# Q's weight load cut into single row chunks, and the fifth column group projected tile by tile

## The chip, the cores and the metric

The kernel runs on one core of a Trainium2 chip. The time is device microseconds (us) of one execution. One execution was also recorded by the hardware profiler; its rows give start and length of every instruction, measured from the first one. The engines are PE (matmuls; PEld is its weight load), DVE (vector), ACT (scalar), POOL (GpSimd) and SP (which here only issues DMA transfers). ACT and POOL can issue transfers too; each issuing engine has its own queue. Every engine works through its own list of instructions in order, and waits on semaphores for the others.

## The reference

One input `x` (2048 rows, 640 columns, bf16) is normalised row by row, and three terms are added:

```python
xn = layernorm(x)                       # (x - mean) / sqrt(var + 1e-5)
# A: attention, 32 heads of 20 columns, window of 8 keys at distance 2
q, k, v = split(xn @ wqkv)              # wqkv: 640 x 1920
logits[h, s, w] = q[h, s] . k[h, s - 2 * w] * 20 ** -0.5    # w = 0..7; s - 2w < 0 is masked
A = (softmax over w of logits, times v[h, s - 2 * w]) @ wo
# B: a bilinear unit
B = ((xn @ w_gate) * (xn @ w_up)) @ w_down                  # 640 x 1536, 1536 x 640
out = x + A + B
```

## The kernel before

**Tiles.** Rows are worked on in 16 tiles of 128 and, in most matmuls, in 4 blocks `j` of 512. The 640 input columns are five row chunks `c` of a weight matrix (128 rows each), and the 640 output columns of Q or K are five column groups `m` of 128 (the columns `m`, `m+5`, ...), so that Q of one tile is 5 x 5 matmuls of 128 columns.

**The normal head.** For tile `t`, `front(t)` makes statistics of the two halves on DVE (L600), the mean and variance (L603), the square root on ACT (L610), its reciprocal on DVE (L617), and the normalised rows `XNS` (L627 on DVE for tiles 0 to 5, L630 on ACT after that). These are transposed to `XNT`: tiles 2 and 3 by PE (L658) and a DVE copy (L664), all others by a transposing DMA (L673). A tile that is ready is marked `xnt`.

**The shortcut for tiles 0 and 1.** To start PE before the normalisation is done, these two tiles are only centred (L695), transposed on PE (L705), copied to `XRAW` by ACT (L716, in two parts: chunks 0 and 1, chunks 2 to 4), and multiplied with Q's and K's weights as they are (`raw_group`, L755, chunk by chunk). The result `RAW` is copied out by ACT (L764) and scaled by row on POOL later (L808).

**The loads at the head** are written out by hand (L1642 to L1655): x of tile 0 in two halves (SP and ACT), x of tile 1, Q's chunks 0 to 2 in one transfer of 480 KB from ACT's queue, Q's chunks 3 and 4 in one of 320 KB from SP's, then K's chunks in two, with x of tiles 2, 3 and 4 between and behind. ACT then loads its table and runs one square root (L1654), and PE runs nine warm-up matmuls (and three more after tile 0's transposes).

**Projections.** `proj_group` multiplies up to four column groups of Q or K for a stretch of rows into one PSUM bank (L838) and lets ACT copy them out (L843). For tiles 2 and 3 the column groups 0 to 3 are done tile by tile; group 4 is done for both tiles together, once for Q and once for K. Then follow V of block 0, and Q, K and V of the later rows. After them come the attention logits (products on DVE L996 and L1045, sums on PE L1128), gate and up (L1430), the weighted values (L1307 on DVE, L1312 on POOL, sums on PE L1366), and the output matmuls (L1531 and L1582).

**What sets the order.** Nothing but the head is ordered by hand. Each piece of work is a `Task` with a priority (smaller is earlier); `Sched.run` keeps an assumed time per engine, takes the assumed cost of each operation (`occ`) and, for the loads at the head, an assumed landing time (`land`), and always emits the task of highest priority among those that could start soon on some engine. `have(...)` holds a chain of tasks until a mark is set. So a changed load, landing time or gate makes the whole order be worked out anew, and each engine's list is fixed when the program is built; on the chip the lists are followed in order whatever the real times are.

Of the kernel before, what the change touches and what calls it, by code (L numbers as in the profile page):

```python
# [11 lines left out]
NCH = 5  # L12
# [9 lines left out]
TS = 128  # L22
# [335 lines left out]
def build_kernel(nc, A_x, A_wqkv, A_wo, B_x, B_w_gate, B_w_up, B_w_down, out):  # L358
    K = Sched(nc)
# [108 lines left out]
    def mark(*k):  # L468
        done.add(k)

    def bump(*k):
        count[k] = count.get(k, 0) + 1

    def have(*k):
        return lambda: k in done
# [7 lines left out]
    def dma(o, i, r=(), w=(), name="", eng="sp", group=None, land=None):  # L483
        n = mybir.dt.size(o.dtype)
        for s in o.shape:
            n *= s
        return op(eng, lambda e: e.dma_start(o, i), r=r, w=w, dma=True, name=name, nbytes=n, group=group, land=land)  # L487
# [27 lines left out]
    def x_load(t, eng="sp", land=None):  # L515
        dma(XST[:, xslot(t), :], xhbm[t * TS:(t + 1) * TS, :], w=[XST[:, xslot(t), :]], name=f"xld{t}", eng=eng, land=land)
        mark("x", t)
# [9 lines left out]
    def wqkv_load(g, lo=0, hi=NCH, eng="sp", land=None):  # L527
        dst = WQKV[:, WPOS[g], lo:hi, :]
        dma(dst, wqkv_src[:, lo:hi, g * D:(g + 1) * D], w=[dst], name=f"ld_wqkv{g}_{lo}", eng=eng, land=land)
# [62 lines left out]
    def front(t):  # L592
# [5 lines left out]
        def stats(i):  # L598
            o, a = st[:, 6 * i:6 * i + 6], x[:, i * DHALF:(i + 1) * DHALF]
            op("dve", lambda e: e.bn_stats(o, a), r=[a], w=[("st", t, i)], name=f"bn{t}_{i}", occ=0.49)  # L600
# [32 lines left out]

        yield have("x", t)
        for i in range(2):
            if t == 4 and i == 1 or t == 5 and i == 0:
                yield have("xnt", 3)
            yield Task("dve", lambda: stats(i), r=[x[:, i * DHALF:(i + 1) * DHALF]] if t == 0 else [x], prio=p)
        yield Task("dve", aggr, r=[("st", t, 1)], prio=p)
# [185 lines left out]
    def wcols(which, c, m):  # L825
        if which == 2:
            return WQKV[:, WPOS[2], c, m * 128:(m + 1) * 128]
        return WQKV[:, WPOS[which], c, m:D:NCH]

    def mms(parts, b, name, outer=None):  # L830
        order = [(p, c) for p in parts for c in range(NCH)]
        if outer is not None:
            order = [(p, c) for c in outer for p in parts]
        for k, ((o, which, m, s0, n), c) in enumerate(order):
            if True:
                first = c == 0
                l, x = wcols(which, c, m), XNT[:, c, s0:s0 + n]
                op("pe", (lambda o, l, x, c, first: lambda e: e.matmul(o, l, x, start=first, stop=(c == NCH - 1)))(o, l, x, c, first),  # L838
                   r=[l, x], w=[o], name=f"{name}_{m}_{c}", occ=n / 2400 + 0.0024, lat=0.3)

    def evac(parts, name):
        for o, i, n in parts:
            X = op("act", (lambda o, i: lambda e: e.activation(o, i, ACT.Copy))(o, i), r=[i], w=[o], name=name,  # L843
                   occ=0.12 + n * 0.9e-3)
        return X

    def qk_dst(which, m0, nm, s0, n):
        if which == 1:
            return KT[:, m0:m0 + nm, PAD + s0:PAD + s0 + n]
        j, i = divmod(s0, JB)  # L850
        return QT[:, j, m0:m0 + nm, i:i + n]

    def bank_view(b, col, nm, n):
        return PS[:, b, col:col + nm * n].rearrange("p (m s) -> p m s", m=nm)

    def proj_group(items, s0, n, prio, keys):
        hold = []

        def go(b):
            parts, outs, col = [], [], 0  # L860
            for which, m0, nm in items:
                for k in range(nm):
                    parts.append((PS[:, b, col + k * n:col + (k + 1) * n], which, m0 + k, s0, n))
                outs.append((qk_dst(which, m0, nm, s0, n), bank_view(b, col, nm, n), nm * n))
                col += nm * n
            mms(parts, b, f"p{items[0][0]}_{s0}")
            hold.append((b, outs))

        def ev():
            b, outs = hold[0]  # L870
            X = evac(outs, f"pev{items[0][0]}_{s0}")
            K.free_bank(b, X)
            for which, m0, nm in items:
                for k in range(nm):
                    for u in range(n // TS):
                        bump("qk", which, (s0 + u * TS) // JB, m0 + k)

        yield Task("pe", go, r=[wcols(items[0][0], NCH - 1, 0), XNT[:, NCH - 1, s0 + n - TS:s0 + n]], prio=prio, banks=1)
        yield Task("act", ev, r=[o for _, o, _ in hold[0][1]], prio=5)

    def proj_qk():
        for t in (2, 3):
            yield have("xnt", t)
            for which in (0, 1):
                K.spawn(proj_group([(which, 0, 4)], t * TS, TS, 10, None))
        for which in (0, 1):
            K.spawn(proj_group([(which, 4, 1)], 2 * TS, 2 * TS, 10.2, None))
        for t in (4, 6):
            yield have("xnt", t + 1)
            for items in ([(0, 0, 2)], [(1, 0, 2)], [(0, 2, 2)], [(1, 2, 2)], [(0, 4, 1), (1, 4, 1)]):  # L890
                if 1 not in QUAD or items[0][0] or items[0][1] == 4:
                    K.spawn(proj_group(items, t * TS, 2 * TS, 11 + t * 0.1, None))
        for j in (2, 3):
            yield have("xnt", 4 * j + 3)
            for m in range(NCH):
                for which in (0, 1):
                    if which or j not in QUAD or m == NCH - 1:
                        K.spawn(proj_group([(which, m, 1)], j * JB, JB, 12 + j, None))
# [743 lines left out]
    x_half(0, 3.05)  # L1642
    x_half(1, 3.25, eng="act")
    x_load(1, land=4.4)
    wqkv_load(0, 0, 3, eng="act", land=5.55)
    wqkv_load(0, 3, NCH, land=6.65)
    wqkv_load(1, 0, 2, land=7.5)
    x_load(2, land=7.95)
    wqkv_load(1, 2, NCH, land=9.3)
    x_load(3, land=9.75)  # L1650
    x_load(4, land=10.2)
    mark("kloads")
    K.t["act"] = 3.0
    op("act", lambda e: e.activation(MV[:, 0, 7:8], EPSC[:, 0:1], ACT.Sqrt), r=[EPSC[:]], w=[("sdx",)], name="table", occ=0.25)  # L1654
    warm(9, JB)  # L1655

# [13 lines left out]
    for t in range(NT):  # L1670
        K.spawn(front(t))
    for t in range(N_RAW):
        K.spawn(raw(t))
    K.spawn(proj_qk())
    K.spawn(products())
    for j in range(NJ):
# [16 lines left out]
def bass_parallel_sum__sliding_local_dilated__glu_gated_bilinear__prompt_kernel(  # L1693
    nc, A_x, A_wqkv, A_wo, B_x, B_w_gate, B_w_up, B_w_down, out
):
    build_kernel(nc, A_x, A_wqkv, A_wo, B_x, B_w_gate, B_w_up, B_w_down, out)
# [28 lines left out]
```

## Time and profile before

| | us |
|---|---|
| median of 3 runs | 264.66 (264.48 to 265.0) |
| profiled execution, its own time | 265.61 |
| its span, first to last instruction | 263.9 |
| PE busy | 259.0 |
| DVE busy | 219.3 |
| POOL busy | 166.5 |
| ACT busy | 112.7 |
| PE's first matmul with Q's weights | 7.14 after the start |

A line of a group names the line of the kernel, the engine, the operation and the tiles (output, then inputs). In the chain of work that ended last, each line is a start, a length and what ran or was waited for; a `q` behind an engine's name is its issuing part. In the list of waits a line says who waited for whom, and then the time in total, how often, and the longest.

### The profile page before, as it was taken

Reading aid. Unit: us, or ns where it says so; the run is one execution under the profiler, and the core shown is the slowest. Engines: PE = TensorE matmul, PEld = TensorE weight load, DVE = VectorE, ACT = ScalarE, POOL = GpSimd, SP = SyncE. Lnnn points to the kernel's source line nnn. Section 1 sums busy time; section 2 is a strip of 40 time slices with the busy share of each in tenths; the row PEclk is TensorE's granted clock in tenths of the full one; section 3 lists DMA queues with packets and bytes.
Section 4 is the critical chain, followed back from the end, with each engine's and each line's share of the span. In section 5 each row is a group of like instructions: output and inputs, shape, how many; then the busy total and the mean of one; then the engine's idle time right before and its main releaser. Section 6 shows DMA issues by size and latency. Waiting matters only on the chain.

```text
span 263.9 us, 4105 instructions
## 1 busy us (share of the span) xinstructions
PE 259.0 (98%) x1586; PEld 135.8 (51%) x1586; DVE 219.3 (83%) x260; ACT 112.7 (43%) x199; POOL 166.5 (63%) x101
## 2 busy tenths in 40 slices
PE   6999999999999999999999999999999999999996
PEld 2996974444444444444444444444444444445675
DVE  5587899999988897679878999999989989995041
ACT  3378988556612221224256855541324116211300
POOL 3017000000599999999983455899979999999300
PEclk9999999999999999999999999999999999999999
DMA  7999689951379995470059532566679865821621
GB/s 222 344 195 171 130 102 387 444 215 36 119 138 190 232 221 106 79 150 11 6 150 322 109 83 50 128 146 178 136 186 188 200 140 138 146 60 35 93 64 50
DMA packets 49387, 40.23 MB, mean 152 GB/s; under 512 B 25144, under 2 KB 47032, under 8 KB 49336
## 3 DMA queue, kind: packets, MB, share of 16 engines
q1 hardware_dynamic: 45944, 33.18, 50.5%
q0 software_dynamic: 2736, 6.16, 13.7%
q10 hardware_dynamic: 688, 0.64, 0.8%
q8 instruction: 12, 0.20, 0.3%
q14 instruction: 7, 0.06, 0.1%
HBM read 25.20 MB, written 7.23 MB: 123 GB/s over the span
## 4 chain that ended last, share of the span: by engine, by line
PE 96%; DMA 2%; ACTq 0%; DVE 0%; issue 0%
PE PS L1430 39%; PE PS L838 23%; PE PS L1531 21%; PE PS L1582 7%; PE PS L755 2%; DMA WQKV<-in_A_wqkv_dram 2%; PE PS L1128 2%; PE PS L1366 2%; PE PS L658 0%; ACTq L487 0%; DVE FB L1595 0%; PE PS L705 0%
## 5 line engine op out<-in xcount | busy, mean ns | idle before, releaser
L1312 POOL TENSOR_TENSOR SV<-PV 128x1024 bf16<-128x1024 f32 x40 | 94.4, 2532 | 17.6 <-DVE LOG L1174 4.4
L1307 DVE TENSOR_TENSOR PV<-VX,PS 128x1024 f32<-128x1024 bf16 (+1 forms) x54 | 90.7, 1727 | 2.8 <-POOL SV L1312 2.8
L838 PE MATMUL PS<-XNT,WQKV 128*128 128x512 bf16 (+2 forms) x390 | 60.7, 316 | 0.0
L1430 PE MATMUL PS<-XNT,WG 128*128 128x512 bf16 x240 | 59.7, 379 | 0.0
L1430 PE MATMUL PS<-XNT,WU 128*128 128x512 bf16 x240 | 59.6, 379 | 0.0
L838 PEld LDWEIGHTS PS<-XNT,WQKV 128*128 128x128 bf16 x390 | 37.9, 112 | 21.9 <-ACT LOG L1139 0.8
L1045 DVE TENSOR_TENSOR PRF<-PS,KT 128x1024 f32<-128x1024 f32 x32 | 37.9, 1215 | 0.3 <-PE PS L838 0.3
L1430 PEld LDWEIGHTS PS<-XNT,WG 128*128 128x128 bf16 x240 | 23.3, 98 | 28.7 <-issue 0.4
L1430 PEld LDWEIGHTS PS<-XNT,WU 128*128 128x128 bf16 x240 | 23.5, 98 | 28.3
L1071 POOL TENSOR_TENSOR PRF<-PRF,PRF 128x1024 f32<-128x1024 f32 x8 | 20.6, 2586 | 21.6 <-DVE LOG L1188 21.6
L843 ACT ACTIVATE HT<-PS 128x512 bf16<-128x512 f32 x24 | 14.4, 599 | 34.9 <-PE PS L1430 34.9
L1531 PE MATMUL PS<-HT,WD 128*128 128x512 bf16 x120 | 27.5, 379 | 0.0
L996 DVE TENSOR_TENSOR PRD<-QT,KT 128x2048 bf16<-128x2048 bf16 x24 | 27.5, 1217 | 0.0
L843 ACT ACTIVATE UX<-PS 128x512 bf16<-128x512 f32 x15 | 9.0, 597 | 41.7 <-PE PS L1531 41.7
L1104 POOL TENSOR_TENSOR PRD<-PRF,PRF 128x1024 bf16<-128x1024 f32 x8 | 20.0, 2611 | 0.0
L1531 PEld LDWEIGHTS PS<-HT,WD 128*128 128x128 bf16 x120 | 11.6, 98 | 14.4 <-ACT OT L1375 0.4
L1082 POOL TENSOR_TENSOR PRF<-PRF,PRD 128x1024 f32<-128x1024 f32 x8 | 18.9, 2482 | 0.0
L1531 PE MATMUL PS<-OT,WO 128*128 128x512 bf16 x75 | 18.6, 379 | 0.0
L1439 DVE TENSOR_TENSOR HT<-HT,PS 128x512 bf16<-128x512 bf16 x18 | 12.3, 685 | 7.2 <-PE PS L1430 7.2
L1595 DVE TENSOR_TENSOR FB<-PS,XR 128x320 bf16<-128x320 f32 (+2 forms) x9 | 4.1, 455 | 16.2 <-PE PS L1582 15.3
L600 DVE BATCH_NORM_STATS2 STATS<-XST 128x6 f32<-128x320 bf16 x32 | 14.2, 467 | 2.9 <-DMA XST<-in_A_x_dram 2.9
L1147 POOL MEMSET LOG<- 32x6 bf16 (+6 forms) x7 | 0.4, 95 | 22.4 <-ACT LOG L1139 22.4
(82 smaller groups left out, 252.5 us busy)
## 6 DMA issues: line engine op xcount, KB each, us to landing
VX<-v_scratch SPq DMA_DIRECT2D x80, 130.0 KB, 3.1
PRF<-PRF POOLq DMA_DIRECT2D x8, 512.0 KB, 5.0
v_scratch<-VST SPq DMA_DIRECT2D x4, 640.0 KB, 6.8
XST<-in_A_x_dram SPq DMA_DIRECT2D x15, 160.0 KB, 5.0
WG<-in_B_w_gate_dram SPq DMA_DIRECT2D x1, 1920.0 KB, 8.4
WU<-in_B_w_up_dram SPq DMA_DIRECT2D x1, 1920.0 KB, 12.6
out_dram<-in_A_x_dram SPq DMA_DIRECT2D x1, 1920.0 KB, 18.6
WD<-in_B_w_down_dram SPq DMA_DIRECT2D x1, 1920.0 KB, 8.7
```

The costliest lines, as they stand in the source:

```text
L838: op("pe", (lambda o, l, x, c, first: lambda e: e.matmul(o, l, x, start=first, stop=(c == NCH - 1)))(o, l, x, c, first), r=[l, x], w=[o], ...
L843: X = op("act", (lambda o, i: lambda e: e.activation(o, i, ACT.Copy))(o, i), r=[i], w=[o], name=name, occ=0.12 + n * 0.9e-3)
L996: op("dve", lambda e: e.tensor_tensor(s[:], qb, kv, ALU.mult), r=[q, rk], w=[s[:]], name=f"prod{j}_{r}_{c}", occ=1.15, lock=True)
L1045: X = op("dve", lambda e: e.tensor_tensor(o[:], qb, kv, ALU.mult), r=[q, rk, ("qev", j, c)], w=[o[:]], name=f"prow{j}_{r}_{c}_{q0}", occ=1.17)
L1071: yield Task("pool", lambda: op("pool", lambda e: e.tensor_tensor(x, x, y, ALU.add), r=[x, y] + tokens(), w=[x], name=name, occ=2.36, lock ...
L1082: yield Task("pool", lambda: op("pool", lambda e: e.tensor_tensor(x, x, z, ALU.add), r=[x, z] + tokens(), w=[x], name=name + "c", occ=2.36 ...
L1104: yield Task("pool", lambda: op("pool", lambda e: e.tensor_tensor(o, a, y, ALU.add), r=[a, y] + tokens(), w=[o], name=f"qend{j}_{r}_{q0}", ...
L1307: last[0] = op("dve", lambda e: e.tensor_tensor(p, vw, a, ALU.mult), r=[vv] + rk, w=[p], name=f"pv{u}_{x}_{r0}", occ=0.09 + 1.1 * nr)
L1312: X = op("pool", lambda e: e.tensor_tensor(o, p[:, :, 0, :], p[:, :, 1, :], ALU.add), r=[p[:]] + tokens(), w=[o], name=f"pva{u}_{x}", occ= ...
L1430: op("pe", (lambda l, x, c: lambda e: e.matmul(PS[:, b, :], l, x, start=(c == 0), stop=(c == NCH - 1)))(l, x, c), r=[l, x], w=[PS[:, b, :] ...
L1531: op("pe", (lambda l, x, i: lambda e: e.matmul(PS[:, b, :], l, x, start=(i == 0), stop=(i == n - 1)))(l, x, i), r=[l, x], w=[PS[:, b, :]], ...
L1582: op("pe", (lambda l, x, i: lambda e: e.matmul(dst, l, x, start=(i == 0), stop=(i == n - 1)))(l, x, i), r=[l, x], w=[PS[:, b, :]], name=f" ...
```

## The change

Three things are altered. Q's row chunks 0, 1 and 2 are loaded by three transfers of 160 KB from ACT's queue and chunks 3 and 4 by two transfers from SP's, each with an assumed landing time of its own; the assumed time at which ACT is free for its table goes from 3.0 to 4.0 with it. The fifth column group of tiles 2 and 3 is projected tile by tile: Q and K of one tile share a bank, as 2 x 5 matmuls of 128 columns, where one matrix for both tiles was 5 matmuls of 256. And the statistics of tiles 6 and 7 wait for the mark of tile 3, as those of tile 5 did.

```diff
@@ front(t)
-            if t == 4 and i == 1 or t == 5 and i == 0:
+            if t == 4 and i == 1 or 5 <= t < 8 and i == 0:
                 yield have("xnt", 3)
@@ proj_qk()
             for which in (0, 1):
                 K.spawn(proj_group([(which, 0, 4)], t * TS, TS, 10, None))
-        for which in (0, 1):
-            K.spawn(proj_group([(which, 4, 1)], 2 * TS, 2 * TS, 10.2, None))
+            K.spawn(proj_group([(0, 4, 1), (1, 4, 1)], t * TS, TS, 10.2, None))
@@ the loads at the head
     x_load(1, land=4.4)
-    wqkv_load(0, 0, 3, eng="act", land=5.55)
-    wqkv_load(0, 3, NCH, land=6.65)
+    wqkv_load(0, 0, 1, eng="act", land=4.75)
+    wqkv_load(0, 1, 2, eng="act", land=5.2)
+    wqkv_load(0, 2, 3, eng="act", land=5.65)
+    wqkv_load(0, 3, 4, land=6.2)
+    wqkv_load(0, 4, NCH, land=6.65)
     wqkv_load(1, 0, 2, land=7.5)
...
     mark("kloads")
-    K.t["act"] = 3.0
+    K.t["act"] = 4.0
```

## The prediction

> **What bounds the kernel now.** I read the engines' busy shares first, then the chain that ended last, then PE's waits.
>
> ```profile
> span 263.9 us, 4105 instructions
> PE 259.0 (98%) x1586; PEld 135.8 (51%) x1586; DVE 219.3 (83%) x260; ACT 112.7 (43%) x199; POOL 166.5 (63%) x101
> ...
> PE 96%; DMA 2%; ACTq 0%; DVE 0%; issue 0%
> ```
>
> TensorE sets the time: 98% busy, 96% of the chain. The DMA share of 2% is one piece. The chain in order of time starts so:
>
> ```profile
> 0.83 0.41 ACTq L487
> 1.24 0.04 issue
> 1.28 5.73 DMA WQKV<-in_A_wqkv_dram
> 7.01 0.14 issue
> 7.14 0.73 PE PS L755 x10
> 7.87 0.11 PE PS L705 x2
> 7.98 0.28 PE PS L755 x5
> 8.26 0.17 PE PS L705 x3
> 8.43 3.35 PE PS L755 x60
> 11.78 0.28 PE PS L658 x5
> 12.06 1.40 PE PS L755 x25
> 13.45 1.12 PE PS L838 x20
> ```
>
> The end hangs on the 480 KB load of Q's row chunks 0 to 2, issued by ACT at 1.28 and landed at 7.01; 0.14 later PE starts, and from there the chain holds practically nothing but PE. PE's own waits say the same:
>
> ```profile
> engine line waited for: us in total, times, longest us
> PE PS L755 <- DMA WQKV<-in_A_wqkv_dram: 1.7, 1, 1.7
> PE PS L822 <- PEq L1710: 0.9, 1, 0.9
> ```
>
> The warm-up matmuls end at 5.41, so the wait is 1.73 us, and after it this view has no further wait of PE. What PE starts earlier at the head can reach the end, if nothing stops it on the way.
>
> **The loads of Q (the first part of the change).** Removed are one issue on ACT's queue (0.45) and one on SP's (0.44), added three and two: ACT +0.9, SP +0.47.
> ACT: its table load (1.28, now at 1.76) and first activation (0.20) move to about 2.7 and end at 4.2; the next work on ACT is the copy of tile 0's raw transposes at 4.83, so 0.6 us of idle hides it. Were that gone, the copy and with it the first Q matmul would be that much later.
> SP: behind the extra issue stand K's two loads and x of tiles 2 to 4, then the store of the row scales at 6.71 (SP is idle from 4.99 until then). These loads wait on data, not on issue: in the window 5.40 to 7.10 the DMA engines were busy 1.05 of their time at 382 GB/s, and x of tiles 3 and 4, issued 0.5 apart, landed 0.45 apart (10.28, 10.73). I take 0 for SP; ends 0 and +0.47.
>
> What matters is when the third chunk lands; call it L. PE takes chunks 0 and 1 first (10 matmuls, 0.56 us by the chain), and behind chunk 2 in PE's in-order queue stand tile 1's raw transposes, the ACT copies that wait for them, and all later matmuls. In the trace chunk 2's matmuls start 0.11 later than that, after two transposes whose input was ready at 6.10; the new order may put these before or behind chunk 2, so I count only the 0.56. Then PE gains 7.14 + 0.56 - (L + 0.14) = 7.56 - L.
> Bounds of L: below, the packet records of the 480 KB load show 15 of the 16 engines writing their completion between 4.57 and 5.17 and the last at 6.60; landing came 0.40 after the last, so L could be 5.57 if that one engine were not late. Above, the SP transfer that was issued at 2.21, when chunk 2 now is (1.28 and two issues of 0.45), landed 5.9 later, at 8.08. The nearest row is the load itself: chunk 2 is the last third of the same 480 KB on the same queue, in competition with the same SP transfers. I take L = 7.01: a gain of 0.55. Chunks 3 and 4 came together at 7.20; in two transfers the second comes no later by this reading, and PE reaches it after L anyway (in the trace chunk 3's matmuls start at 8.26, chunk 4's at 8.82), so: 0.
>
> Further limits on the gain, if L is early. Chunk 4 at 7.20 + 0.14 against 8.82: 1.48 at most. K's chunks 2 to 4 land at 9.85, used at 11.33: 1.34. Tile 2's transposes on PE at 11.61 need the normalised rows that DVE finished at 10.87; x of tile 2 lands at 8.53, its statistics end at 9.69, and the square root started at 9.90 behind ACT's evacuation of 9.30 to 10.01. With that evacuation earlier the chain could be 0.18 earlier, so transposes at 10.73: a gain of 0.88 at most, or 1.16 if the new order puts five more raw matmuls (0.28) ahead of them. So 1.16 is the most the head can give. Tile 3 follows: its transposes (14.40) trail DVE's copy of tile 2 (12.09) by 2.31, and that copy itself waits for PE, so it moves along; its copy ends 0.42 before PE needs it.
>
> **The fifth column group by tile.** Removed: two groups of five matmuls 256 wide, PE from 18.03 to 19.13, 1.10 us. Added: 20 matmuls 128 wide, at 20 in 1.12 us (the last line of the chain above): +0.02 on PE. What it offers is 0.56 us of work on tile 2 that no longer waits for tile 3; in the trace PE had no gap there to fill, so 0, and at most 0.5 if tile 3 becomes late. On ACT two evacuations (0.39, 0.38) become four. 512 columns take 0.60 and 256 take 0.385, so 128 take about 0.28 (an estimate from these two): 1.11 - 0.77 = +0.34. ACT is idle 2.1 of the 6 us from 14 to 20, which hides it. Without that cover the nearest bank reuse on PE is a matmul at 36.52 whose bank ACT emptied at 35.11: 1.4 us of slack, which covers 0.34 and 0.55 together.
>
> **The statistics of tiles 6 and 7 held for tile 3.** In the trace they start at 16.93 and later, behind tile 3's copy (14.88 to 15.37). Nothing to hold: 0. Ends: minus 0.48 (one such instruction out of tile 3's way) and plus 0.48 (DVE idle where one could have run).
>
> **From the head to the end.** The same work follows on PE, so a gain stops only at inputs less than it ahead. V's first matmul (19.13) had its input at 16.42, tiles 4 and 5 (24.52) at 22.45; the four batches of sums had their last addition 3.5, 4.8, 2.5 and 2.2 us before its matmul. All exceed 1.16, even if DVE and POOL did not move at all. Sum: -0.55 + 0.02 = -0.53. The profiled execution takes 265.61 (its span 263.9 and 1.7 around), so 265.08 on its own clock; it lies 0.95 above the median of the runs, 264.66. Taken from that median: 264.1.
>
> **Where a rule speaks against it.** Row: x of tile 1, 160 KB on SP, took 3.35 from issue to landing, yet transfers queued behind each other land 0.45 apart. If three transfers of one queue did not overlap at all, chunk 2 would land at 1.28 + 3 x 3.35 = 11.3 and the time would be 268.4; the 0.45 spacing all but excludes that, and I give it 0.01, counted in rival C. The Trainium skill, "DMA: Bandwidth & Descriptors", section "Rules for kernel authors", advises few large transfers; its section "Anatomy of one DMA" (fitted on GpSimd's path) gives each a fixed 2.0 us. By its figures in series (an estimate from that page) three would land at 1.28 + 3 x 2.4 = 8.4, and the sum would be 265.5.
>
> **The rivals.**
> A, more: the one late engine is not late for small transfers. L up to 6.7 suffices; then tile 2's chain decides, 0.88 to 1.16 less 0.02: 263.5 to 263.8. For it: 15 of 16 engines. Against it: on an engine that serves both queues in turn, chunk 2 still shares with SP's loads.
> B, no change: the profiled run is 0.95 slower than the timed ones, and that is what an earlier landing of the 480 KB would be worth: PE would then stop at chunk 3 until 7.20 + 0.14 = 7.34 instead of 8.26, which is 0.92. If the timed runs have no late engine, they already stand at tile 2's limit of 0.88, and only the 0.28 of order is left: 264.4 to 264.7. Against it: the 0.95 can as well lie outside the span.
> C, slower: chunk 2, third on ACT's queue, is served in order of issue with SP's loads, behind them. It decides from L = 7.56 on. With the row of equal issue time, L = 8.08: +0.52 + 0.02, so 265.2. Against it: ACT's queue holds 560 KB up to chunk 2, just as much as SP's did up to the load that landed at 7.20.
>
> **How the numbers follow.** The forecast (264.1, its own range 263.9 to 264.4) has 0.38, A 0.20, B 0.25, C 0.17 (in it 0.01 for loads in series and 0.04 for an unlucky new order further on). 0.2% is 0.53 us, about what a measurement of this kernel tells from no change. Faster by more: A and somewhat over half of the forecast, 0.43. Within: the rest of the forecast and most of B, 0.38. Slower: C and a little of B, 0.19. The range leaves out A's lower part and C's upper: 263.5 to 265.1.
>
> **What would show it.** Right: three ACT loads of 160 KB landing one after another, the last near 7.0; PE's wait of 1.73 broken into shorter ones with ten matmuls done before the last; tile 2's first projection (13.29) near 12.75; the last sums (246.59) near 246.05; no new wait on PE after 13. A: projection at 12.1 to 12.4 and a PE wait on DVE before tile 2's transposes. B: the same trace, but timed runs that do not follow it. C: a wait on WQKV that ends after 7.7. Wrong altogether: a PE wait after 14, on ACT's evacuations or tile 3's copy.

## The result

The changed kernel takes 265.45 us (median of 9 runs, 264.95 to 266.4), the kernel before 264.44 on the same chip (9 runs, 264.09 to 265.19). The ratio is 1.004, 95% interval [1.0022, 1.0057]: slower by about 1.0 us. The forecast was 264.1, faster by about 0.5.

The page of the kernel after begins so (span; busy time and instructions by engine; the chain that ended last, by engine):

```profile
span 263.5 us, 4107 instructions
PE 258.0 (98%) x1575; PEld 136.2 (52%) x1596; DVE 219.6 (83%) x260; ACT 112.7 (43%) x201; POOL 166.5 (63%) x101
...
PE 95%; DMA 2%; ACT 1%; issue 1%; ACTq 1%; DVE 0%
```

PE is as full as before. Some of its matmul records are missing from this trace (1575, with 1596 weight loads). That is where the chain's new pieces of ACT and "issue" come from: in after_again, a second trace of the same kernel with all 1596, they are gone. The beginning of the chain, in order of time (start, length, what):

```profile
2.23 4.69 DMA WQKV<-in_A_wqkv_dram
6.93 0.14 issue
7.06 0.45 PE PS L755 x5
7.51 0.11 PE PS L705 x2
7.62 0.28 PE PS L755 x5
7.90 0.17 PE PS L705 x3
8.07 3.35 PE PS L755 x60
11.42 0.28 PE PS L658 x5
11.70 1.12 PE PS L755 x20
12.82 2.23 PE PS L838 x40
15.05 0.28 PE PS L658 x5
15.33 0.56 PE PS L838 x10
15.89 0.03 issue
```

The head hangs on chunk 2, the third of ACT's transfers: issued at 2.23, landed at 6.93. Tile 2 now has 40 projections in one piece where it had 20 before tile 3's transposes. PE's waits (who waited for whom; total, times, longest) show chunk 2 again, 0.7 where it was 1.7. The three lines behind it stand where records are missing, and after_again doesn't have them:

```profile
PE PS L822 <- PEq L1712: 0.9, 1, 0.9
PE PS L755 <- DMA WQKV<-in_A_wqkv_dram: 0.7, 1, 0.7
PE PS L838 <- issue: 0.4, 2, 0.2
PE PS L1429 <- ACT LOG L1138: 0.2, 1, 0.2
PE PS L1429 <- issue: 0.2, 1, 0.2
```

On the timeline (start, length, engine, line, operation and tiles; in brackets the idle time before and what ended it) PE does ten matmuls early and then waits:

```profile
5.63 0.72 PE L755 MATMUL PS<-XRAW,WQKV 128*128 128x128 bf16 x10
7.06 0.45 PE L755 MATMUL PS<-XRAW,WQKV 128*128 128x128 bf16 x5 [0.72 <-DMA WQKV<-in_A_wqkv_dram]
12.65 2.40 PE L838 MATMUL PS<-XNT,WQKV 128*128 128x128 bf16 x40
```

Read alone, this is what the prediction wanted: L, the landing of chunk 2, at 6.93 for 7.01 forecast, the first projection of tile 2 at 12.65 (by the timeline, where every piece keeps its own start) for about 12.75 forecast, and a span 0.4 shorter, 263.5 for 263.9. The profiled execution of after takes 265.28, close to its median. That of before, 265.61, is above every one of the 77 timed runs of before in this study (264.04 to 265.24). So the question was which of the two before-traces the timed runs resemble, and what the change really costs against that.

### The profile page after: what moved, and what is told of

The parts are those of the page before. It is cut to its first block, busy times and chain, and to the rows that moved or that the text cites. A ratio compares the mean times of both kernels' runs of the same rounds, so it can differ in the third digit from the quotient of the medians.

```text
span 263.5 us, 4107 instructions
## 1 busy us (share of the span) xinstructions
PE 258.0 (98%) x1575; PEld 136.2 (52%) x1596; DVE 219.6 (83%) x260; ACT 112.7 (43%) x201; POOL 166.5 (63%) x101
## 3 DMA queue, kind: packets, MB, share of 16 engines
q0 software_dynamic: 2736, 6.16, 13.6%
## 4 chain that ended last, share of the span: by engine, by line
PE 95%; DMA 2%; ACT 1%; issue 1%; ACTq 1%; DVE 0%
PE PS L1429 38%; PE PS L838 23%; PE PS L1530 21%; PE PS L1581 7%; PE PS L755 2%; PE PS L1127 2%; PE PS L1365 2%; DMA WQKV<-in_A_wqkv_dram 2%; ACTq L487 1%; ACT LOG L1138 0%; ACT XNT L843 0%; ACT HX L843 0%; PE PS L658 0%; ACT PS L1264 0%; ACT UF L843 0%
## 5 line engine op out<-in xcount | busy, mean ns | idle before, releaser
L1429 PE MATMUL PS<-XNT,WG 128*128 128x512 bf16 x235 | 58.6, 379 | 0.4 <-ACT LOG L1138 0.2
L1429 PE MATMUL PS<-XNT,WU 128*128 128x512 bf16 x235 | 58.6, 379 | 0.4 <-issue 0.2
L1070 POOL TENSOR_TENSOR PRF<-PRF,PRF 128x1024 f32<-128x1024 f32 x8 | 23.0, 2885 | 21.8 <-DVE LOG L1187 21.8
L1103 POOL TENSOR_TENSOR PRD<-PRF,PRF 128x1024 bf16<-128x1024 f32 x8 | 21.4, 2911 | 0.1
L1081 POOL TENSOR_TENSOR PRF<-PRF,PRD 128x1024 f32<-128x1024 f32 x8 | 20.8, 2685 | 0.0
L843 ACT ACTIVATE VST<-PS 128x512 bf16<-128x512 f32 x20 | 11.6, 594 | 8.4 <-PE PS L838 8.4
```

The costliest lines, as they stand in the source:

```text
L1070: yield Task("pool", lambda: op("pool", lambda e: e.tensor_tensor(x, x, y, ALU.add), r=[x, y] + tokens(), w=[x], name=name, occ=2.36, lock ...
L1081: yield Task("pool", lambda: op("pool", lambda e: e.tensor_tensor(x, x, z, ALU.add), r=[x, z] + tokens(), w=[x], name=name + "c", occ=2.36 ...
L1103: yield Task("pool", lambda: op("pool", lambda e: e.tensor_tensor(o, a, y, ALU.add), r=[a, y] + tokens(), w=[o], name=f"qend{j}_{r}_{q0}", ...
L1429: op("pe", (lambda l, x, c: lambda e: e.matmul(PS[:, b, :], l, x, start=(c == 0), stop=(c == NCH - 1)))(l, x, c), r=[l, x], w=[PS[:, b, :] ...
```

## The experiments

Every kernel below computes the whole result. In the table, "start of tile 2" is the start of its first projection in the profiled execution; "rest" is the span less that. The time of an execution is its span and 1.7 to 1.8 around it, in all of them.

| kernel | ratio to before, 95% | chunk 2 lands | first Q matmul | start of tile 2 | span | rest |
|---|---|---|---|---|---|---|
| before (the trace shown) | | 7.01 | 7.14 | 13.29 | 263.9 | 250.6 |
| before_again | | 5.40 | 5.82 | 12.21 | 262.8 | 250.6 |
| sp_split_only | 0.9998 [0.9988, 1.0008] | 5.60 | 5.74 | 11.89 | 262.5 | 250.6 |
| act_split_only | 1.0039 [1.0026, 1.0052] | 7.67 | 5.69 | 13.28 | 263.9 | 250.6 |
| split_old_order | 1.0032 [1.0019, 1.0045] | 6.51 | 5.38 | 12.37 | 263.0 | 250.6 |
| need_order | 1.0011 [0.9997, 1.0025] | 5.58 | 5.82 | 12.54 | 263.1 | 250.6 |
| need_order_x2 | 0.9996 [0.9986, 1.0007] | 5.52 | 5.82 | 12.26 | 262.8 | 250.6 |
| x2_first | 0.9995 [0.9986, 1.0004] | 6.03 | 6.16 | 12.31 | 262.9 | 250.6 |
| new_order_old_loads | 1.0021 [1.0012, 1.003] | 6.05 | 6.19 | 12.62 | 263.5 | 250.9 |
| order_only | 1.0017 [1.0005, 1.003] | 5.62 | 5.76 | 11.90 | 262.9 | 251.0 |
| after | 1.004 [1.0022, 1.0057] | 6.93 | 5.63 | 12.65 | 263.5 | 250.9 |
| after_again | 1.0056 [1.0041, 1.007] | 6.78 | 5.70 | 12.51 | 263.4 | 250.9 |
| after_no_gate | 1.005 [1.0037, 1.0063] | 7.63 | 5.82 | 13.36 | 264.2 | 250.8 |

The last column is the first finding: with before's order of work 250.6 follow the start of tile 2, whatever the head did, and with a new order 250.8 to 251.0. What the head wins or loses reaches the end undiminished, as the prediction had it, and the new order costs 0.25 to 0.45 behind the head.

### The kernel before once more

No edit. Expected:

> The kernel before, unchanged, profiled once more. Theory 1 (the profile of before shown was an unusual execution, in which one DMA engine was late): here the 480 KB load of Q lands between 5.6 and 6.3 instead of 7.01, PE's first matmul with Q's weights is at 5.8 to 6.4 instead of 7.14, and the span is 262.4 to 263.2 instead of 263.9. Theory 2 (the head of before is always as shown, and the new order of the work costs the time): landing near 7.0 again, span 263.7 to 264.1. Theory 3 (the 0.95 between the shown profile and the median lies outside the span): span 263.9, time 264.4.

The profiled execution takes 264.52 (timed runs on that chip: median 264.2). On the timeline PE's first Q matmuls and the start of tile 2, here and then in before:

```profile
5.82 0.96 PE L755 MATMUL PS<-XRAW,WQKV 128*128 128x128 bf16 x10
12.21 0.78 PE L838 MATMUL PS<-XNT,WQKV 128*128 128x128 bf16 x11
```

```profile
7.14 0.45 PE L755 MATMUL PS<-XRAW,WQKV 128*128 128x128 bf16 x5 [1.73 <-DMA WQKV<-in_A_wqkv_dram]
13.29 1.28 PE L838 MATMUL PS<-XNT,WQKV 128*128 128x128 bf16 x20
```

The same 480 KB transfer, issued at 1.27 here and at 1.28 there, landed at 5.40 here and at 7.01 there. By the packet records all 16 DMA engines had written their completion by 5.00 here, where in before one engine wrote its own at 6.60. The 1.73 that the change was to shorten isn't there in this execution: PE goes from its warm-up matmuls to Q without a pause. The transfer is early in the other four kernels that keep it whole, too (5.60, 5.62, 6.03, 6.05), and PE's longest idle time ahead of Q is 0.64 in them. The median agrees: 264.44 less 1.75 around the span less 250.6 puts the start of tile 2 at 12.1.

### The two halves of the change apart

split_old_order has the five transfers with before's assumed landing times, so that PE, DVE and ACT keep before's order of work; new_order_old_loads has the changed order with before's two transfers.

```diff
# split_old_order, against before
-    wqkv_load(0, 0, 3, eng="act", land=5.55)
-    wqkv_load(0, 3, NCH, land=6.65)
+    wqkv_load(0, 0, 1, eng="act", land=5.55)
+    wqkv_load(0, 1, 2, eng="act", land=5.55)
+    wqkv_load(0, 2, 3, eng="act", land=5.55)
+    wqkv_load(0, 3, 4, land=6.65)
+    wqkv_load(0, 4, NCH, land=6.65)
# new_order_old_loads, against after
-    wqkv_load(0, 0, 1, eng="act", land=4.75)
-    wqkv_load(0, 1, 2, eng="act", land=5.2)
-    wqkv_load(0, 2, 3, eng="act", land=5.65)
-    wqkv_load(0, 3, 4, land=6.2)
-    wqkv_load(0, 4, NCH, land=6.65)
+    wqkv_load(0, 0, 3, eng="act", land=4.75)
+    wqkv_load(0, 3, NCH, land=6.65)
...
-    K.t["act"] = 4.0
+    K.t["act"] = 3.0
```

> Only the five transfers instead of two, with the old assumed landing times, so that PE, DVE and ACT keep the instructions of before in the order of before. Theory 1 (before usually has its 480 KB load by about 6, and the split makes chunk 2 land near 6.9 every time): slower than before by 0.3 to 0.8 us, chunk 2 at 6.7 to 7.1. Theory 2 (the order costs it): faster by 0.3 to 0.6, or the same. Theory 3 (all of the loss is in the transfers): slower by 0.8 to 1.2.

> The changed kernel with Q's loads in the two old transfers (assumed landing of the first 4.75, ACT's table time 3.0 again); PE's order is that of the changed kernel but for three transposes of tile 1, which come before chunk 3's five matmuls, and DVE's is the same. Theory 1: slower than before by 0.3 to 0.7 us, through tile 3's transposes, which now stand behind 40 projection matmuls of tile 2 instead of 20. Theory 2: slower by 0.9 to 1.4. Theory 3: the same as before.

> The changed kernel once more, beside the others on one chip. All theories: slower than before by 0.7 to 1.3 us. Theory 1: the two parts measured apart sum up to this within 0.3, and chunk 2 lands at 6.7 to 7.1 again.

Measured: 265.05, 264.74 and 265.96, with before at 264.2 (19 runs) on that chip. Both halves cost: +0.85 for the transfers, +0.55 for the order, 1.4 together. after_again, the changed kernel unedited, is at +0.56%, 1.5, more than the 0.7 to 1.3 that was expected; the result above was 0.4%, the two intervals overlap, and which is nearer isn't settled. The five transfers cost slightly more than the 0.3 to 0.8 of theory 1, with chunk 2 slightly earlier than its 6.7.

The sum of the halves fits better than it should. In new_order_old_loads tile 1's five transposes stand behind 15 matmuls in one piece, and the weight loads of the matmuls behind them wait for ACT's copy:

```profile
7.84 0.66 PEld L755 LDWEIGHTS PS<-XRAW,WQKV 128*128 128x128 bf16 x11 [0.18 <-ACT XRAW L716]
```

That 0.2 is no part of after's cost: there the transposes stand in two pieces, and neither trace of it has such a wait. Behind the head it has after's 0.3.

The landings show what five transfers do. By issue (time) and landing in split_old_order: chunk 0, ACT (1.27) 4.67; chunk 3, SP (1.73) 5.62; chunk 1, ACT (1.75) 5.84; chunk 4, SP (2.20) 6.20; chunk 2, ACT (2.23) 6.51. That is the order of issue over both queues, and chunk 2, which PE needs third, comes last. On the timeline of split_old_order three things hold PE up: chunk 1 (the ten matmuls take 0.98 where after has 0.72), chunk 2, and tile 2's transposes, whose rows came late (PE stands 0.2 at 10.69, by its starts):

```profile
5.38 0.98 PE L755 MATMUL PS<-XRAW,WQKV 128*128 128x128 bf16 x10
6.65 0.45 PE L755 MATMUL PS<-XRAW,WQKV 128*128 128x128 bf16 x5 [0.17 <-DMA WQKV<-in_A_wqkv_dram]
10.69 0.45 PE L658 MATMUL PS<-IDENT,XNS 128*128 128x128 bf16 x5
```

The bytes of the two queues in the stretch from 3.3 to 4.4 show what changed (queue, kind: packets, MB, share of the engines; q10 is ACT's, q1 is SP's), first before_again, then split_old_order:

```profile
q10 hardware_dynamic: 264, 0.34, 83.0%
q1 hardware_dynamic: 66, 0.07, 17.4%
```

```profile
q1 hardware_dynamic: 161, 0.19, 53.2%
q10 hardware_dynamic: 167, 0.19, 48.0%
```

As one transfer, chunks 0 to 2 get five parts in six of what is moved; as three, half. The total is nearly the same (0.41 and 0.38 MB in 1.1 us). In after the parts are 0.19 and 0.16. The Trainium skill, "DMA: Bandwidth & Descriptors", section "Queues, rings and completion order", says that an engine which has work from several queues takes a packet from each in turn: the even shares of the split loads agree, the 0.34 to 0.07 of the whole one doesn't follow from it, and no run here shows what gives the long transfer its lead.

### Which of the two splits costs

```diff
# sp_split_only, against before
-    wqkv_load(0, 3, NCH, land=6.65)
+    wqkv_load(0, 3, 4, land=6.65)
+    wqkv_load(0, 4, NCH, land=6.65)
# act_split_only, against before
-    wqkv_load(0, 0, 3, eng="act", land=5.55)
+    wqkv_load(0, 0, 1, eng="act", land=5.55)
+    wqkv_load(0, 1, 2, eng="act", land=5.55)
+    wqkv_load(0, 2, 3, eng="act", land=5.55)
```

> Chunks 0 to 2 in the one old transfer from ACT, chunks 3 and 4 in two from SP, order of all engines as before. Theory I (transfers of both queues are served about in the order of issue, so that chunk 2, issued last, comes last): chunks 0 to 2 land first, between 5.3 and 6.2, and the time is that of before within 0.3 us. Theory S (every further transfer costs by itself): slower by 0.2 to 0.4, about half of the 0.85 that the full split cost.

> Chunks 0, 1 and 2 in three transfers from ACT, chunks 3 and 4 in the one old transfer from SP, order of all engines as before. Theory I: SP's transfer, issued second, lands before chunk 2, which lands at 6.4 to 7.0; slower than before by 0.5 to 1.0 us. Theory S: slower by 0.4 to 0.6, with chunk 2 before SP's chunks 3 and 4.

Measured: 264.31 and 265.65, with before at 264.49 (28 runs). SP's split is free; ACT's costs all of it. On the timeline of act_split_only PE has chunks 0 and 1 early and then stands until the last piece:

```profile
5.69 0.84 PE L755 MATMUL PS<-XRAW,WQKV 128*128 128x128 bf16 x10
6.37 0.28 PE L705 MATMUL PS<-IDENT,XCT 128*128 128x128 bf16 x2
7.80 0.45 PE L755 MATMUL PS<-XRAW,WQKV 128*128 128x128 bf16 x5 [1.16 <-DMA WQKV<-in_A_wqkv_dram]
```

Chunk 2 landed at 7.67, later than the 6.4 to 7.0 that theory I expected, and SP's 320 KB of chunks 3 and 4 at 6.35: the piece that is needed first came after the ones that are needed later. A price by transfer, which theory S had, falls: sp_split_only has one more and costs nothing.

The early chunk 0 (4.43) gains little. PE starts at 5.69 and in before_again, with the whole load, at 5.82: behind its own warm-up matmuls and ACT's copy of tile 0's transposes, the first part of which ends at 5.49 in both. Where the whole load lands later than 5.40, it does set PE's start: sp_split_only and order_only begin 0.14 after it.

```profile
5.74 0.73 PE L755 MATMUL PS<-XRAW,WQKV 128*128 128x128 bf16 x10
5.76 0.73 PE L755 MATMUL PS<-XRAW,WQKV 128*128 128x128 bf16 x10
```

But with an early chunk 0 the start is hardly sooner, 5.38 to 5.82 in the seven executions that have one.

### Issued in the order of need, and the order of work alone

need_order keeps five transfers and before's order of work, but issues the chunks in the order in which PE takes them, from the two queues in turn. order_only has before's loads and assumed landings with the other two parts of the change.

```diff
# need_order, against before
+    wqkv_load(0, 0, 1, eng="act", land=5.55)
+    wqkv_load(0, 1, 2, land=5.55)
+    wqkv_load(0, 2, 3, eng="act", land=5.55)
+    wqkv_load(0, 3, 4, land=6.65)
+    wqkv_load(0, 4, NCH, eng="act", land=6.65)
# order_only, against before
-            if t == 4 and i == 1 or t == 5 and i == 0:
+            if t == 4 and i == 1 or 5 <= t < 8 and i == 0:
...
-        for which in (0, 1):
-            K.spawn(proj_group([(which, 4, 1)], 2 * TS, 2 * TS, 10.2, None))
+            K.spawn(proj_group([(0, 4, 1), (1, 4, 1)], t * TS, TS, 10.2, None))
```

> The same five transfers as in the full split, but issued in the order in which PE needs them: chunks 0, 2 and 4 from ACT, 1 and 3 from SP, order of all engines as before. Theory I: they land in the order 0, 1, 2, 3, 4, chunk 2 at 5.5 to 6.2; faster than the full split by 0.5 to 1.0 us, so between 0.2 faster and 0.3 slower than before. Theory S: as slow as the full split, 0.7 to 1.0 behind before.

> Before's loads and assumed landing times, with the other two parts of the change: the fifth column group tile by tile, and the statistics of tiles 6 and 7 behind tile 3. Tile 3's transposes keep their place behind 20 projections of tile 2. If the 0.55 us that the new order cost came from tile 3's transposes standing behind 40 of them (which the earlier assumed landings brought about): same as before within 0.25 us. If it came from these two parts themselves: slower by 0.4 to 0.7.

Measured: 264.88, ratio 1.0011 with an interval that includes 1, and 264.86, 1.0017, which is the 0.4 to 0.7 of "these two parts themselves". In need_order the chunks land at 4.31, 5.40, 5.58, 6.58 and 7.08, and PE waits for none of them. It waits one step further on (the list of waits):

```profile
PE PS L658 <- DVE XNS L627: 0.3, 1, 0.3
```

Tile 2's rows are normalised late because x of tile 2 landed at 8.63, a whole us after the 7.64 of before_again. So chunk 2's wait had only been covering the next one.

In order_only the head is as early as any (11.90), and PE stops later, on the timeline:

```profile
33.39 0.82 PE L838 MATMUL PS<-XNT,WQKV 128*128 128x512 bf16 x3 [0.23 <-ACT XNS L630]
```

The new order reaches a projection before its rows are there (the transposing DMA of tile 11, issued at 29.03, landed at 33.30); before had no such wait. By the starts of the matmuls PE loses 0.39 there, nearly all of the 0.45 by which this kernel's rest is longer. That one transfer took 4.27 where the same tile's took 2.68 in before_again; whether the new order makes it slow or chance does, one trace can't say. In after the wait is another one. The view of tile XNT in after, 14 to 17 us, with DVE's copy of tile 3 and who waited for it:

```profile
L664 DVE COPY XNT<-PS x1: 492/492/492, 15.4 to 15.4; 128x640 bf16<-128x640 bf16 x1
...
  PEld PS L838: 0.2, 1
```

PE takes tile 3's transposes only after all 40 projections of tile 2 (the chain above, 15.05), has ten matmuls left to do while DVE copies for 0.49, and stops 0.2. That is most of the 0.3 by which after's rest is longer, and in after_again, by the starts of all its matmuls, it is the only stop behind the start of tile 2. The 40 come only where the assumed landings are changed too: in order_only, with the column group and the gate alone, tile 3's transposes keep their place behind 20. So a new order costs by waits, and each order has its wait at another place.

### Closing the last wait, and the gate

need_order_x2 is need_order with x of tile 2 issued ahead of K's first two chunks; x2_first is before with that swap alone; after_no_gate is after without the gate.

```diff
# need_order_x2, against need_order; x2_first, against before
-    wqkv_load(1, 0, 2, land=7.5)
     x_load(2, land=7.95)
+    wqkv_load(1, 0, 2, land=7.5)
# after_no_gate, against after
-            if t == 4 and i == 1 or 5 <= t < 8 and i == 0:
+            if t == 4 and i == 1 or t == 5 and i == 0:
```

> Five single-chunk loads of Q issued in the order in which they are needed, from the two queues in turn, as before, and now x of tile 2 issued ahead of K's first two chunks; every engine's order of work is that of the kernel before. My theory: with five transfers in the needed order what was left was tile 2's chain (PE stood 0.47 at its transposes because x of tile 2 landed at 8.6). With x of tile 2 at about 7.7 that stop goes, the start of tile 2's first projection is 12.0 to 12.2 after the start and the time is that of the kernel before: ratio 0.998 to 1.0005. Rival: the extra small transfers themselves cost, or K's first two chunks, now later by one x, stop PE instead: then the start stays at 12.4 or more and the ratio at 1.001 to 1.003.

> The kernel before with one change: x of tile 2 is issued ahead of K's first two chunks. My theory: in the usual execution of the kernel before PE doesn't wait for tile 2 (the start of its first projection follows from PE's first Q matmul at 5.7 to 5.9 alone), so nothing is gained: ratio 0.999 to 1.001. Rival: in the timed runs tile 2's chain is often the limit; then 0.998 or less. K's first two chunks land at about 8.0 instead of 7.2 and are needed at about 8.6: no wait, unless the 480 KB load is early.

> The changed kernel without the gate: statistics of tiles 6 and 7 may run ahead of tile 3's copy again. The built order then has two of tile 6's statistics on DVE ahead of tile 3's copy. My theory (the later order costs because tile 3's copy comes just too late for PE): that copy ends up to 0.9 later, PE's wait of 0.19 at its projections grows to 0.5 to 1.1, ratio 1.006 to 1.010. Rival: DVE has time to spare there, the gate does nothing, and the ratio is that of the changed kernel, 1.004 to 1.006.

Measured: 264.18, 264.42 and 265.85, with before at 264.47 (21 runs). need_order_x2 is before's time with five transfers: x of tile 2 landed at 7.22, the stop of 0.3 is gone, tile 2 starts at 12.26. That closes the account of the loads: what they cost was the order of landing, not their number. Nothing is won by them either, with chunk 0 there at 4.34: PE starts at 5.82, right behind its warm-up matmuls. x2_first is level with before too, so tile 2's rows are not what limits before's usual execution. In x2_first, PE did wait for the whole 480 KB (it landed at 6.03, and PE began at 6.16), and still ended with the others:

```profile
6.16 0.73 PE L755 MATMUL PS<-XRAW,WQKV 128*128 128x128 bf16 x10 [0.64 <-ACT MV L610]
12.31 1.28 PE L838 MATMUL PS<-XNT,WQKV 128*128 128x128 bf16 x20
```

The releaser named there, an ACT square root that no Q matmul reads, is wrong: the landing 0.13 before is what PE waited for, at the same distance as in before (7.01 and 7.14).

after_no_gate went against my theory. Two statistics did run ahead of tile 3's copy, and the copy wasn't late for it. DVE in after_no_gate, then in after:

```profile
14.49 0.88 DVE L600 BATCH_NORM_STATS2 STATS<-XST 128x6 f32<-128x320 bf16 x2
16.07 0.49 DVE L664 COPY XNT<-PS 128x640 bf16<-128x640 bf16 x1 [0.69 <-PE PS L658]
```

```profile
15.37 0.49 DVE L664 COPY XNT<-PS 128x640 bf16<-128x640 bf16 x1 [1.48 <-PE PS L658]
```

The copy starts when PE's transposes are done; with the gate DVE stands idle 1.48 before it, without it 0.69, and PE's wait is 0.2 either way. Tile 3's copy is late because PE takes the transposes late. The gate is thus not what costs in after. No kernel here has the column group alone or the assumed landings alone, so what each of them does by itself stays open. The ratio, 1.005, is that of the changed kernel; the longer span of its profile (264.2) is chunk 2 at 7.63.

## Why the prediction was wrong

**The step that failed** is the base of the sum: "Taken from that median: 264.1". The 0.53 was worked out on an execution whose 480 KB load landed at 7.01, and then taken off a median of executions that usually have it early (5.40 in before_again, 5.60 to 6.05 in the four other kernels that keep it whole). Against the profiled execution the sum was nearly right (263.9 to 263.5, -0.4 for -0.53). Against the usual head (12.1 by the median) that of the three profiles of the changed loads and order, 12.51 to 13.36, is later by 0.4 to 1.3. By the same subtraction after's median (265.45, with its rest of 250.9) puts its start of tile 2 at 12.8: of the 1.0 that the change costs, some 0.7 lies in the head and 0.3 behind it (an estimate from the two medians and the table). The premise of rival B was true: the 0.95 that the profiled run lay above the median was its late landing. The argument against it, that the 0.95 may lie outside the span, falls with the 1.7 to 1.8 around the span in every execution. B then put no price on the split itself.

**L = 7.01** was right for after (6.93, 6.78), by a reading that was wrong. The nearest row was not the late 480 KB load, but rival C's: service in the order of issue over both queues, which the landings of the five single chunks show in all four executions of that split, with 6.5 to 7.6 in place of C's 8.08. C's threshold of 7.56 is measured from the late before-trace. Against a PE that starts at 5.7 to 5.8, does ten matmuls (0.56 by the starts) and turns to chunk 2 at 6.2 to 6.4, any L above some 6.2 costs.

**Chunks 3 and 4: 0.** True of SP's split alone (0.9998). But they are what chunk 2 queues behind when ACT's load is split. The sum priced each split by itself.

**ACT's issues and its +0.34, hidden:** the issues were: ACT's first activation ends at 4.21 in after, 4.2 in the prediction, and its next copy starts at 5.11. The 0.34 was not tried alone; in after_again PE has no wait for it. **SP's extra issue, between 0 and +0.47, taken as 0:** sp_split_only bears out 0.

**The fifth group, +0.02, and "at most 0.5 if tile 3 becomes late":** tile 3 did become late, by 0.2, because the new order puts all 40 projections of tile 2 ahead of its transposes. "It moves along" assumed before's order of those lists. A PE wait after 14 on tile 3's copy was the prediction's own sign of being wrong altogether, and it came. Measured for the new order: 0.45 (order_only) to 0.55 (new_order_old_loads, with 0.2 of its own at the head), of which 0.45 and 0.3 stand in the profiled executions behind the head. This was 0.04 of rival C and should have been a rival of its own.

**The gate: 0,** right in its size, for after: without it tile 3's copy still starts when PE's transposes are done, and PE's wait is the same. In order_only it was not tried.

**From the head to the end:** right; the column "rest" of the table holds to within 0.03 for one order of work.

**The rule on few large transfers.** The Trainium skill, "DMA: Bandwidth & Descriptors", section "Rules for kernel authors", advises few large transfers, and the direction came out so: the 265.5 that the prediction estimated from the same page's fixed 2.0 us ("Anatomy of one DMA") is by luck about the time measured. A fixed price in series isn't what the runs show: one more transfer on SP cost 0.0, and with three more in the order of need the ratio was 1.0011 and, with x of tile 2 ahead, 0.9996.

## What to carry to other kernels

Before a wait in one profiled execution is counted as a gain, ask whether the timed runs have it: a profiled run that lies above all of them may owe that to the very wait, and the sum must start from their head, not from its own. Here cutting a load took away its lead over the other queue, and the single chunks landed in the order of issue over both queues: issue them in the order of need, and look at what then lands later (here x of the next tile). Where an order is worked out anew by a planner, price that by itself; here it cost 0.3 to 0.45 behind the head.

## What was not expected of the hardware

The landing of one transfer, the same 480 KB issued at 1.26 to 1.28, varied from 5.40 to 7.01 between two executions of one kernel, and lay between these in four kernels more. In these six executions the start of tile 2 lies between 11.9 and 13.3, further apart than the 1.0 that the change costs.

One transfer of 480 KB got 0.34 of the 0.41 MB moved between 3.3 and 4.4 us, while three of 160 KB got 0.19 of 0.38, and 0.20 of 0.35 next to the same uncut 320 KB load (act_split_only).

The first ten Q matmuls take 0.73 in some executions and 0.96 in others, by the two lines of x2_first and before_again above; in the latter the starts of the first five are 0.106 apart instead of 0.056, at a granted clock that the profile gives as 1.00.
